# First product in float16 parts: split on ScalarE and VectorE, transposed by DMA, with the chunk's x norm in the taps

## The chip, the cores and the metric

The kernel runs on one core of a Trainium2 chip. The metric is the device time of one execution in microseconds (us), lower is better. Before the change it is 1389.54 us, the median of three runs (1389.52 to 1389.61).

## What is computed

`x` is 8 × 4160 rows of 192 floats, `weight_gen` holds 8 heads × 7 taps for each row. The two stages, cut to what matters:

```
# stage 1: a causal convolution of 7 taps with softmaxed weights, by head (24 columns each)
w   = softmax(weight_gen over its 7 taps)
att[s, head] = sum over k of w[s, head, k] * x[s - 6 + k, head]

# stage 2: two products with a normalized, self-gated softmax between them
h    = att @ w_in                       # 33280 x 192 times 192 x 1024
solu = h * exp(h - max(h)) / (sum(exp(h - max(h))) + 1e-9)
ln   = (solu - mean(solu)) / sqrt(var(solu) + 1e-6) * g_ln
out  = ln @ w_out                       # 1024 x 192
```

`w_in` and `w_out` arrive as 64-bit floats and are made into 32-bit ones on the chip.

## The kernel before

Each of the 128 partitions owns a run of 260 consecutive rows. A *tile* is one row of every partition, so there are 260 tiles of 128 rows. The taps and x are loaded by *chunks* of 4, 8, 8 and then 16 tiles.

**Stage 1** works on *groups* of four tiles (the first two groups have two). GpSimd (POOL) multiplies the seven shifted rows by their taps (L133), adds three pairs (L139) and then two pairs into `half` (L141). VectorE (DVE) adds the last two into `a` (`fin`, L366). The softmax of a chunk's taps has seven steps t0 to t6: DVE maximum (L112), POOL subtraction (L114), ScalarE (ACT) exponential (L118), DVE sum (L120), ACT and DVE for the reciprocal (L122, L124), POOL product (L126).

**The way into the first product**, by pairs of tiles: ACT doubles the last 64 columns of `a` (`dup`, L372). TensorE (PE) transposes four 128×128 blocks against an identity into the PSUM buffer `pa` (`xT`, L383). ACT rounds them to fp32r, a 32-bit type that PE multiplies in one pass (`xhi`, L391). What rounding lost, `x_lo`, is made for every other pair by a PE product with minus the identity and an ACT copy (`xn` L398, `xlo` L405), and for the other pairs by one DVE subtraction (`xld`, L412).

**The first product** of a tile (`mm1`) is twelve matmuls of 512 columns in fp32r: high × high, high × low and low × high, six with 128 rows (L422) and six with 64 rows that go in twos beside each other (L427). Its result `h`, 128 × 1024 in PSUM, has three buffers.

**Between the products**, for each tile: DVE takes the negated maximum (`max`, L441), a bound (`vb`, L445) and its reciprocal (`vr`, L450); ACT the exponential with its sum (`exp`, L454); DVE h × scale × exp with its mean (`solu`, L460); ACT the squares (`sq`, L466) and the float16 high half (`hi`, L473); DVE the float16 low half (`lo`, L477). Per four tiles, eight short steps f0 to f7 on ACT and DVE (L500 to L520) make the factor of the output rows. One DMA then transposes the two halves of a tile, 16 blocks of 128×128 (`tr`, L485).

**The second product** (`mm2`, L529) is 24 matmuls of 192 columns in float16; ACT scales the result out of PSUM (`out`, L540), and every four tiles are stored (L543).

**What sets the order.** Every engine executes its instructions in the order in which they are written. `issue_order` (L603) writes that order before anything runs: a list of steps with an engine, a cost in nanoseconds and the steps that they wait for, run through a small schedule in which each engine takes the step with the lowest tile number plus `URGENCY`. So an engine waits where a step's input comes later than that schedule had it. All DMAs are issued by SyncE (SP), in order too, through one queue. POOL can run ahead of the rest by as much as the buffers hold: `half` has two, `a` three groups.

Of the kernel before, what the change touches and what calls it, by code (L numbers as in the profile page):

```python
# [12 lines left out]
I32 = mybir.dt.int32  # L13
# [13 lines left out]
def tile_kernel(ctx: ExitStack, tc: tile.TileContext, x, weight_gen, w_in, w_out, g_ln, out):  # L27
# [17 lines left out]
    FH = FF // 2  # L45

# [53 lines left out]
    TAP_STEPS = 7  # L100

    def softmax_taps(c, step):
# [54 lines left out]
    ident = const.tile([P, P], F32, name="ident")  # L157
    make_identity(nc, ident)
# [74 lines left out]

    def first_rows(f, step):
        fs = slice(f * FH, (f + 1) * FH)
        if step < 3:
            first[f] = float_of_double(f, raw_a[:, f * FF : (f + 1) * FF], FH, step)
        elif step == 3:
            nc.scalar.copy(wa_hi[:, fs], first[f])
        elif step == 4:  # L240
            nc.vector.tensor_tensor(
                out=wa_lo[:, fs], in0=first[f], in1=wa_hi.bitcast(F32)[:, fs], op=ALU.subtract
            )
# [41 lines left out]
    def prepare_second(step, half=None):  # L285
# [8 lines left out]
        elif step == 5:  # L294
            second["total"] = ps_a.tile([P, 512], F32, name="pa")
            nc.tensor.matmul(second["total"][:, :NP], ones, sq, start=True, stop=True)
        elif step == 6:

            total = second["total"]
            tot = total[:, 8:9]  # L300
            k, kinv = (total.bitcast(I32)[:, n : n + 1] for n in (9, 10))
            nc.vector.tensor_reduce(tot, total[:, :NP], axis=AX.X, op=ALU.add)
            nc.vector.tensor_scalar(
                k, tot.bitcast(I32), 1, EXPONENT,
                op0=ALU.logical_shift_right, op1=ALU.bitwise_and,
            )
# [22 lines left out]
    a_of = {}  # L329
# [28 lines left out]
    def columns(t):  # L358
        return a_of[t // TG][:, t % TG : t % TG + group(t), :]

    def last_sum(t):
        if t % TG == 0:

            a_of[t // TG] = att.tile([P, TG, 2 * P], F32, name="a", bufs=3)
        half = half_of.pop(t)
        nc.vector.tensor_reduce(  # L366
            columns(t)[:, :, :D], half.rearrange("p j t d -> p t d j"), axis=AX.X, op=ALU.add
# [475 lines left out]
```

## Time and profile before

| | |
|---|---|
| Median of three runs | 1389.54 us |
| The profiled execution: its time, its span | 1389.4 us, 1387.5 us |
| Granted TensorE clock, mean | 0.991 |
| Busy: PE, POOL, DVE, ACT | 91%, 90%, 89%, 81% |
| DMA: bytes, mean rate | 210.43 MB, 152 GB/s |

The profile is of one execution. Its span starts with the first and ends with the last instruction; the execution's time is 1.9 us longer. An instruction's *busy* time runs from its start to its end; on DVE and ACT the last hundredths of a microsecond of one overlap the start of the next, and on PE the ends are modelled. *Idle before* a group of instructions is time in which its engine stood still ahead of them, with the instruction or DMA that ended it (the *releaser*). PEld is the load of weights into PE, which overlaps PE.

### The profile page before, as it was taken

To read this page: it belongs to the slowest core of one execution; us is meant where nothing else is said; L and a number is where in the kernel's file an instruction comes from. 1 tells how busy PE (TensorE), PEld (TensorE's weight loads), DVE (VectorE), ACT (ScalarE), POOL (GpSimd) and SP (SyncE) were. 2 spreads that over 40 slices of the span, in tenths; PEclk is the share of its full clock that TensorE was granted. 3 is DMA by queue.
4 is the path that set the end of the run, shared out by engine and by line. 5 is a ranking of instruction groups with operands and counts; after the bars stand their busy time and mean duration, and the time that the engine had idled before them with its cause. 6 is when DMAs were issued, how large, how long until landed. Compare 5 with 4: busy or idle time off the path is not lost.

```text
span 1387.5 us, 26562 instructions
## 1 busy us (share of the span) xinstructions
PE 1259.2 (91%) x10028; PEld 988.6 (71%) x10028; DVE 1230.0 (89%) x2068; ACT 1128.5 (81%) x2231; POOL 1247.0 (90%) x243
## 2 busy tenths in 40 slices
PE   0389899999999999989989999999999999999997
PEld 0267677777777777767767677777777777777776
DVE  2999898999989899889989898989899889999984
ACT  1588887888888888888888888888788888888885
POOL 1999999999999999999999999999999999999100
PEclk9989999999999999999999999999999999999999
DMA  3469768696968789697857768687858668766765
GB/s 90 139 142 194 147 128 201 124 207 122 194 130 174 146 145 195 122 198 123 186 130 166 158 149 186 118 190 145 193 109 191 146 140 176 132 133 117 134 131 116
DMA packets 565241, 210.43 MB, mean 152 GB/s; under 512 B 544329, under 2 KB 545785, under 8 KB 565112
## 3 DMA queue, kind: packets, MB, share of 16 engines
q1 hardware_dynamic: 565112, 208.73, 72.5%
q8 instruction: 79, 1.29, 0.4%
q14 instruction: 50, 0.41, 0.1%
HBM read 46.19 MB, written 25.56 MB: 52 GB/s over the span
## 4 chain that ended last, share of the span: by engine, by line
POOL 51%; DVE 16%; issue 13%; ACT 13%; PE 4%; DMA 3%; SPq 0%; POOLq 0%; DVEq 0%; ACTq 0%
POOL pr L133 27%; POOL pr L139 15%; POOL half L141 6%; DVE h L460 5%; ACT hl L473 4%; DVE hl L477 4%; ACT e L466 3%; DVE stats L441 3%; ACT e L454 3%; DVE a L366 3%; DMA xt<-in_x_dram 2%; POOL wt L114 2%; PE po L529 2%; POOL wt L126 1%; PE h L422 1%
## 5 line engine op out<-in xcount | busy, mean ns | idle before, releaser
L133 POOL TENSOR_TENSOR pr<-xt,wt 128x5376 f32<-128x5376 f32 (+1 forms) x66 | 631.3, 9565 | 23.1 <-DMA xt<-zeros 20.5
L529 PE MATMUL po<-w_hl,hlT 128*128 128x192 f16 x6192 | 558.5, 247 | 26.6 <-ACT ot L540 26.2
L529 PEld LDWEIGHTS <-hlT 128*128 128x128 f16 x6240 | 515.2, 98 | 82.2 <-issue 79.2
L477 DVE SCALAR_TENSOR_TENSOR hl<-h,hl 128x1024 f16<-128x1024 f32 x260 | 315.4, 1220 | 44.2 <-ACT e L466 31.5
L460 DVE SCALAR_TENSOR_TENSOR h<-h,stats,e 128x1024 f32<-128x1024 f32 x260 | 334.7, 1288 | 22.4 <-ACT e L454 9.2
L473 ACT ACTIVATE hl<-h 128x1024 f16<-128x1024 f32 x260 | 267.3, 1028 | 92.3 <-DVE stats L497 57.4
L139 POOL TENSOR_TENSOR pr<-pr 128x2304 f32<-128x2304 f32 (+1 forms) x66 | 332.7, 5041 | 5.2
L441 DVE TENSOR_REDUCE stats<-h 128x1 f32<-128x1024 f32 x260 | 316.1, 1216 | 8.9 <-PE h L427 8.1
L454 ACT ACTIVATE e<-h,stats 128x1024 f32<-128x1024 f32 x260 | 292.6, 1126 | 31.1 <-DVE stats L441 27.2
L466 ACT ACTIVATE e<-h,stats 128x1024 f32<-128x1024 f32 x260 | 292.3, 1125 | 5.9 <-DVE hl L477 5.4
L422 PE MATMUL h<-wa_hi,x_hi 128*128 128x512 f32 x520 | 225.4, 433 | 36.3 <-ACT e L466 22.8
L141 POOL TENSOR_TENSOR half<-pr 128x1536 f32<-128x1536 f32 (+1 forms) x66 | 225.8, 3422 | 5.2
L422 PE MATMUL h<-wa_hi,x_lo 128*128 128x512 f32 x520 | 207.5, 399 | 0.8 <-ACT x_lo L405 0.8
L422 PE MATMUL h<-wa_lo,x_hi 128*128 128x512 f32 x520 | 206.3, 397 | 0.0
L422 PEld LDWEIGHTS h<-wa_hi,x_hi 128*128 128x128 f32 x520 | 98.9, 190 | 59.3 <-ACT e L466 26.0
L427 PE MATMUL h<-wb_hi,x_hi 64*128 64x512 f32 x520 | 131.1, 500 | 0.0
L383 PE MATMUL pa<-ident,a 128*128 128x128 f32 x520 | 84.6, 286 | 44.2 <-DVE a L366 44.1
L540 ACT ACTIVATE ot<-po,stats 128x192 f32<-128x192 f32 x258 | 111.4, 432 | 8.5 <-PE po L529 8.5
L366 DVE TENSOR_REDUCE a<-half 128x768 f32<-128x1536 f32 (+1 forms) x66 | 116.4, 1764 | 1.6 <-POOL half L141 1.6
L427 PEld LDWEIGHTS h<-wb_hi,x_hi 64*128 64x128 f32 x520 | 48.6, 184 | 96.7 <-issue 96.7
L422 PEld LDWEIGHTS h<-wa_hi,x_lo 128*128 128x128 f32 x520 | 98.6, 190 | 24.3 <-ACT x_lo L405 1.6
L383 PEld LDWEIGHTS pa<-ident,a 128*128 128x128 f32 x520 | 55.8, 142 | 79.7 <-DVE a L366 44.1
(79 smaller groups left out, 1194.1 us busy)
## 6 DMA issues: line engine op xcount, KB each, us to landing
out_dram<-ot SPq DMA_DIRECT2D x65, 384.0 KB, 3.3
xt<-in_x_dram SPq DMA_DIRECT2D x30, 576.0 KB, 4.7
xt<-in_x_dram SPq DMA_DIRECT2D x30, 480.0 KB, 4.7
wt<-in_weight_gen_dram SPq DMA_DIRECT2D x15, 448.0 KB, 4.1
hlT<-hl SPq DMA_TRANSPOSE x260, 4.5
raw<-in_moe_w_out_dram SPq DMA_DIRECT2D x1, 1536.0 KB, 9.4
xt<-in_x_dram SPq DMA_DIRECT2D x3, 384.0 KB, 6.0
raw_a<-in_moe_w_in_dram SPq DMA_DIRECT2D x2, 512.0 KB, 11.5
```

What stands on the lines that cost most here:

```text
L133: nc.gpsimd.tensor_tensor(out=window(pr, 0, [(TG * D, K), (HG, n * H), (1, HG)]), in0=window(xt, t * D, [(D, K), (HG, n * H), (1, HG)]), i ...
L139: nc.gpsimd.tensor_tensor(out=pr[:, :3], in0=pr[:, :3], in1=pr[:, 3:6], op=ALU.add)
L141: nc.gpsimd.tensor_tensor(out=half, in0=window(pr, 0, [(2 * TG * D, 2), (D, n), (1, D)]), in1=window(pr, TG * D, [(5 * TG * D, 2), (D, n), ...
L422: nc.tensor.matmul(h[:, fs], lhs[:, 0, :], rhs[:, fs], start=n == 0, stop=False)
L427: nc.tensor.matmul(h[:, fs], lhs[rows, 1, :], rhs[rows], start=False, stop=n == 2,)
L441: nc.vector.tensor_reduce(stat(t, NMAX), h_of[t], axis=AX.X, op=ALU.max, negate=True)
L454: nc.scalar.activation(e, h_of[t], AF.Exp, bias=stat(t, NMAX), accum_out=stat(t, Z))
L460: nc.vector.scalar_tensor_tensor(out=h, in0=h, scalar=stat(t, SIGMA), in1=e, op0=ALU.mult, op1=ALU.mult, accum_out=stat(t, M))
L466: nc.scalar.activation(e_of.pop(t), h_of[t], AF.Square, bias=stat(t, M), scale=-float(FF), accum_out=stat(t, Q),)
L473: nc.scalar.activation(hl[:, 0, :], h_of[t], AF.Copy, scale=2.0**14)
L477: nc.vector.scalar_tensor_tensor(out=hl[:, 1, :], in0=h_of[t], scalar=2.0**14, in1=hl[:, 0, :], op0=ALU.mult, op1=ALU.subtract,)
L529: nc.tensor.matmul(po[:, :D], hlT[:, half * NJ + j, :], w2_hl[:, j, w, :], start=n == 0, stop=n == len(terms) - 1,)
```

## The change

**The first product in float16.** `att` is scaled by 2^14 and split into a float16 high and low part, and so is `w_in`, by a power of two found from the sum of its squares. The low × low part is dropped. High and low columns of a tile lie beside each other as 384 columns, three blocks of 128: the 64 last high columns share a block with the first 64 low columns, so that ten matmuls of 512 columns with 128 rows each are the whole product.

```
-        for fs in halves:
-            for n, (lhs, rhs) in enumerate(((hi, wa_hi), (hi, wa_lo), (lo, wa_hi))):
-                nc.tensor.matmul(h[:, fs], lhs[:, 0, :], rhs[:, fs], start=n == 0, stop=False)
...
+        terms = [(0, wa_hi), (0, wa_lo), (1, wb_hi), (1, wb_lo), (2, wc_hi)]
+        for f in range(2):
+            fs = slice(f * FH, (f + 1) * FH)
+            for n, (b, rhs) in enumerate(terms):
                 nc.tensor.matmul(
+                    h[:, fs], x3[:, b, :], rhs[:, fs], start=n == 0, stop=n == len(terms) - 1
                 )
```

**The way into it.** `fin` now writes a pair of tiles into PSUM (`pa`, one buffer); ACT writes the high part, DVE the low part, and one DMA on SP's queue transposes the six blocks of a pair into `xT` (four buffers). `dup`, the PE transposes, `xn`, `xlo` on ACT and `xld` are gone.

```
+        nc.vector.tensor_reduce(
+            pa, half.rearrange("p j t d -> p t d j"), axis=AX.X, op=ALU.add
+        )
+        part_of[t] = pa, small.tile([P, 2, 2 * D], F16, name="xhl", bufs=2)
+
+    def high_x(t):
+        pa, xhl = part_of[t]
+        nc.scalar.activation(xhl[:, :, :D], pa, AF.Copy, scale=S_UNIT)
+
+    def low_x(t):
+        pa, xhl = part_of[t]
+        nc.vector.scalar_tensor_tensor(
+            out=xhl[:, :, D:], in0=pa, scalar=S_UNIT, in1=xhl[:, :, :D],
+            op0=ALU.mult, op1=ALU.subtract,
+        )
...
+        nc.sync.dma_start_transpose(xT, xhl.rearrange("p t d -> p (t d)"))
```

**The norm of x.** So that float16 holds them, the taps of a chunk are divided by the root of the sum of squares of the chunk's x and of the chunk before (per partition). ACT squares a chunk's x in four instructions of 768 elements (L149; one for a short chunk), DVE adds (L155), ACT makes the power −1/2 by Ln and Exp (L160, L161), and a new step t6 multiplies it into the taps' reciprocal on ACT (L128), ahead of the POOL product, which is now t7 (L130). The factor back is `BACK`, used as the scale of `exp` and `solu`.

```
+            nc.scalar.activation(
+                junk[:, : (r1 - r0) * D].rearrange("p (t d) -> p t d", d=D), rows, AF.Square,
+                accum_out=squares_x[:, c + 1, part : part + 1],
+            )
...
+            nc.scalar.activation(row[:, LN], row[:, SUM], AF.Ln, bias=floor)
+            nc.scalar.activation(row[:, SIG], row[:, LN], AF.Exp, scale=-0.5)
```

**The row scale comes later.** ACT makes `SHIFT` = maximum × `BACK` (`nb`, L486) between `max` and `exp`; `vb` reads it, and the row's scale `vr` goes into `hi` and `lo` (until now 2^14) and no longer into `solu`. Of the steps per four tiles, six are left.

```
+    def shift(t):
+        nc.scalar.activation(stat(t, SHIFT), stat(t, NMAX), AF.Copy, scale=row(t, BACK))
...
-            out=h, in0=h, scalar=stat(t, SIGMA), in1=e, op0=ALU.mult, op1=ALU.mult, accum_out=stat(t, M)
+            out=h, in0=h, scalar=row(t, BACK_S), in1=e, op0=ALU.mult, op1=ALU.mult,
+            accum_out=stat(t, M),
...
-        nc.scalar.activation(hl[:, 0, :], h_of[t], AF.Copy, scale=2.0**14)
+        nc.scalar.activation(hl[:, 0, :], h_of[t], AF.Copy, scale=stat(t, SIGMA))
```

**The preparation of `w_in`** gets a sum of squares (ACT), a PE product and four short DVE steps for the power of two, and nine DMAs that put the rows of the blocks together, ahead of the first `mm1`.

**The order.** `URGENCY` is another table, and the steps have other costs and waits; among them:

```
-    a00=-79.4, a01=-110.4, a02=-10.4, a03=-9.5, a04=28.3, a10=35.2, a11=8.2, a12=-10.4, a13=2,
+    a00=-24.8, a01=-1.4, a02=311.9, a03=-96.8, a04=-123, a05=-44.2, a06=161.9, a10=70.9, a11=29.9,
...
-        add("attA", t, POOL, 14206 if full else 7302, *after, ready=21100 if c == 1 else 0)
-        add("attB", t, POOL, 3380 if full else 1764, ("attA", t), ("fin", groups[i - 2] if i > 1 else -1))
+        add("attA", t, POOL, 14990 if full else 7500, *after, ready=21100 if c == 1 else 12000)
+        done = [(f"fin", u + 2 if group(u) == 4 else u) for u in groups[i - 2 : i - 1] if i > 1]
+        add("attB", t, POOL, 3480 if full else 1800, ("attA", t), *done)
```

What this does to the order is shown at three places. Of the numbers behind a name, the higher is the buffer that was taken later in the written program.

First ACT at the start, where `w_in` (h, 128x512), the taps of the first chunks (wt 128x224 and 128x448, wy) and now their x (xt) are worked on. Before:

```order
L201 ACTIVATE h<-h 128x512
L202 ACTIVATE h<-h 128x512
L118 ACTIVATE wt<-wt 128x224
L122 ACTIVATE wy<-wm 128x32
L201 ACTIVATE h<-h 128x512
L202 ACTIVATE h<-h 128x512
L228 CAST wb_hi<-h 128x512
```

Now:

```order
L239 ACTIVATE h<-h 128x512
L240 ACTIVATE h<-h 128x512
L149 ACTIVATE junk,squares_x<-xt 128x1920
L120 ACTIVATE wt<-wt 128x224
L239 ACTIVATE h<-h 128x512
L240 ACTIVATE h<-h 128x512
L282 ACTIVATE e,sq<-h 128x512
L160 ACTIVATE row<-row,floor 128x1
L161 ACTIVATE row<-row 128x1
L124 ACTIVATE wy<-wm 128x32
L149 ACTIVATE junk,squares_x<-xt 128x1536
L128 ACTIVATE wy<-wy,row 128x32
```

The first chunk's tap scale (L128) now stands behind the squares of the x of chunk 0 (1920 elements) and of chunk 1 (1536 elements); before, nothing of the taps of chunk 0 stood behind a load of x.

Second POOL's last group (tiles 256 to 259), and DVE's maxima whose h buffer was taken just before and just after that group's `half`. Before, POOL and then DVE:

```order
L133 TENSOR_TENSOR pr_14931<-xt_13329,wt_12372 128x5376
L139 TENSOR_TENSOR pr_14931<-pr_14931 128x2304
L141 TENSOR_TENSOR half_14930<-pr_14931 128x1536
...
L441 TENSOR_REDUCE stats_129<-h_14865 128x1
L460 SCALAR_TENSOR_TENSOR h_14807,stats_129<-h_14807,stats_129,e_14882 128x1024
...
L441 TENSOR_REDUCE stats_129<-h_14935 128x1
```

Now:

```order
L172 TENSOR_TENSOR pr_14881<-xt_13222,wt_12282 128x5376
L178 TENSOR_TENSOR pr_14881<-pr_14881 128x2304
L180 TENSOR_TENSOR half_14880<-pr_14881 128x1536
...
L483 TENSOR_REDUCE stats_121<-h_14861 128x1
L507 SCALAR_TENSOR_TENSOR h_14809,stats_121<-h_14809,row_13584,e_14874 128x1024
...
L483 TENSOR_REDUCE stats_121<-h_14928 128x1
```

Before, h_14865 is the maximum of the 239th tile, so that 21 tiles' products are written behind POOL's last group; now h_14861 is the 250th, and 10 are. Counted the same way at tile 20 these leads are 9 and 10: before, POOL's lead grows through the program, now it stays.

Third DVE in the middle of the program, the work of two tiles. Before:

```order
L460 SCALAR_TENSOR_TENSOR h,stats<-h,stats,e 128x1024
L497 TENSOR_REDUCE stats<-stats 128x4
L441 TENSOR_REDUCE stats<-h 128x1
L477 SCALAR_TENSOR_TENSOR hl<-h,hl 128x1024 x2
L445 TENSOR_REDUCE stats<-stats 128x1
L412 TENSOR_TENSOR x_lo<-pa,x_hi 128x512
L450 RECIPROCAL stats<-stats 128x1
L460 SCALAR_TENSOR_TENSOR h,stats<-h,stats,e 128x1024
L497 TENSOR_REDUCE stats<-stats 128x4
```

Now:

```order
L483 TENSOR_REDUCE stats<-h 128x1
L490 TENSOR_REDUCE stats<-stats 128x1
L495 RECIPROCAL stats<-stats 128x1
L507 SCALAR_TENSOR_TENSOR h,stats<-h,row,e 128x1024
L483 TENSOR_REDUCE stats<-h 128x1
L436 TENSOR_REDUCE pa<-half 128x384
L525 SCALAR_TENSOR_TENSOR hl<-h,stats,hl 128x1024
L545 TENSOR_REDUCE stats<-stats 128x4
L490 TENSOR_REDUCE stats<-stats 128x1
L507 SCALAR_TENSOR_TENSOR h,stats<-h,row,e 128x1024
L495 RECIPROCAL stats<-stats 128x1
```

`fin` (L436) comes by pairs, in smaller pieces; `solu` (L507) no longer needs the reciprocal (L495) ahead of it, and `vb` (L490) now needs ACT's `nb` between it and the maximum (L483).

More of the change, by code (lines that the diff above doesn't have):

```diff
@@ new lines, in scale_first @@
+    def scale_first(step):
+        if step == 0:
+            first["total"] = ps_o.tile([P, 512], F32, name="po")
+            nc.tensor.matmul(first["total"][:, :3], ones, sq[:, 4:7], start=True, stop=True)
+        elif step == 1:
+            exponents(first["total"], 3)
+        elif step == 2:
+            k = first["k"] = small.tile([P, 1], F32, name="k", bufs=2)
+            nc.scalar.copy(k, first["total"][:, 9:10])
+            for n, factor in enumerate((1.0, S_UNIT)):
+                nc.scalar.activation(
+                    back[:, n : n + 1], first["total"][:, 10:11], AF.Copy, scale=factor
+                )
@@ L377, in transpose_x @@
     def transpose_x(t):
-        a = a_of[t // TG]
-        pa = ps_a.tile([P, 2, 2, P], F32, name="pa")
+        _, xhl = part_of.pop(t)
+        xT = small.tile([P, 6, P], F16, name="xT", bufs=4)
+        nc.sync.dma_start_transpose(xT, xhl.rearrange("p t d -> p (t d)"))
         for i in range(2):
-            for n in range(2):
-                nc.tensor.matmul(
-                    pa[:, n, i, :], a[:, (t + i) % TG, n * P : (n + 1) * P], ident,
-                    is_transpose=True, start=i == n == 0, stop=i == n == 1,
-                )
@@ L387, in transpose_x @@
-        x_parts[t] = [pa]
-    def high_x(t):
-        hi = small.tile([P, 2, 2, P], F32R, name="x_hi", bufs=2)
-        nc.scalar.copy(hi, x_parts[t][0])
-        x_parts[t].append(hi)
-    def subtract_high(t):
-        pa, hi = x_parts[t]
-        for n in range(2):
-            nc.tensor.matmul(
-                pa[:, n], minus, hi[:, n], start=False, stop=n == 1, skip_group_check=True
-            )
-    def low_x(t):
-        pa, hi = x_parts.pop(t)
-        lo = small.tile([P, 2, 2, P], F32R, name="x_lo", bufs=2)
-        nc.scalar.copy(lo, pa)
-        for i in range(2):
-            xt_of[t + i] = hi[:, :, i, :], lo[:, :, i, :]
@@ L554, in tile_kernel @@
     ops = dict(
-        attA=attend, attB=lambda t: None, fin=last_sum, dup=copy_columns, xT=transpose_x,
-        xhi=high_x, xn=subtract_high, xlo=low_x, xld=low_x_on_vector, mm1=first_product,
-        max=maximum, vb=bound, vr=row_scale, exp=exponentials, solu=solu, sq=squares, hi=high_half, lo=low_half,
-        tr=transpose_s, mm2=second_product, out=finish, od=store, lw=at_chunk(load_w),
-    )
-    for n in range(5):
-        ops[f"b{n}"] = once(last_rows, n)
-    for n in range(5):
-        for f in range(2):
-            ops[f"a{f}{n}"] = once(first_rows, f, n)
+        attA=attend, attB=lambda t: None, fin=last_sum, xhi=high_x, xlo=low_x, xT=transpose_x,
+        mm1=first_product, max=maximum, nb=shift, vb=bound, vr=row_scale, exp=exponentials,
+        solu=solu, sq=squares, hi=high_half, lo=low_half, tr=transpose_s, mm2=second_product,
+        out=finish, od=store, lw=at_chunk(load_w),
+    )
+    for part in range(3):
+        for n in range(7):
+            ops[f"a{part}{n}"] = once(convert_first, part, n)
+    for n in range(3):
+        ops[f"s{n}"] = once(scale_first, n)
     for n in range(3):
```

340 lines of the change are left out of this document (190 added, 150 removed).

## Prediction

> **What bounds the kernel now.** I read the page's sum first, then the span cut into stages, then the groups of instructions between 300 and 1200 us, where nothing of the start or the end is left.
>
> ```profile
> PE 1259.2 (91%) x10028; PEld 988.6 (71%) x10028; DVE 1230.0 (89%) x2068; ACT 1128.5 (81%) x2231; POOL 1247.0 (90%) x243
> ```
> ```profile
> 300.00:600.00 300.00, 286.34 (x2308) 225.02 (x2305) 277.13 (x462) 255.36 (x503) 296.94 (x56) 1.00 0.79 159
> 600.00:900.00 300.00, 282.56 (x2268) 221.51 (x2267) 272.77 (x454) 251.20 (x494) 297.02 (x55) 0.99 0.75 156
> 900.00:1200.00 300.00, 286.43 (x2291) 225.25 (x2290) 273.44 (x459) 254.42 (x502) 296.78 (x54) 0.99 0.75 158
> 1290.00:1340.00 50.00, 49.32 (x396) 38.50 (x395) 44.27 (x78) 42.34 (x86) 0.00 (x0) 1.00 0.65 122
> ```
> ```profile
> L141 POOL TENSOR_TENSOR half<-pr 128x1536 f32<-128x1536 f32 x47 | 163.2, 3472 | 3.7
> L441 DVE TENSOR_REDUCE stats<-h 128x1 f32<-128x1024 f32 x178 | 216.3, 1216 | 3.5 <-PE h L427 2.9
> L118 ACT ACTIVATE wt<-wt 128x896 f32<-128x896 f32 x11 | 10.5, 952 | 30.3 <-POOL wt L114 30.3
> L366 DVE TENSOR_REDUCE a<-half 128x768 f32<-128x1536 f32 x47 | 84.2, 1791 | 1.6 <-POOL half L141 1.6
> L412 DVE TENSOR_TENSOR x_lo<-pa,x_hi 128x512 fp32r<-128x512 f32 x45 | 30.7, 682 | 0.3 <-ACT x_hi L391 0.2
> L497 DVE TENSOR_REDUCE stats<-stats 128x4 f32<-128x8 f32 (+1 forms) x179 | 28.0, 157 | 11.9 <-ACT stats L516 5.4 <-ACT e L466 3.7 <-ACT stats L500 2.1
> L391 ACT CAST x_hi<-pa 128x512 fp32r<-128x512 f32 x89 | 52.6, 591 | 3.4 <-PE pa L383 3.4
> L405 ACT CAST x_lo<-pa 128x512 fp32r<-128x512 f32 x44 | 26.3, 598 | 0.6 <-PE pa L398 0.5
> L372 ACT COPY a<-a 128x256 f32<-128x256 f32 x47 | 19.4, 413 | 11.0 <-DVE a L366 10.9
> L504 ACT ACTIVATE stats<-stats 128x4 f32<-128x4 f32 x45 | 9.3, 208 | 1.1 <-DVE stats L497 1.1
> ```
>
> In a window the columns behind its length are the busy times of PE, PEld, DVE, ACT and POOL. In these 900 us POOL is busy 890.7 (99%), PE 855.3 (95%), DVE 823.3 (91%), ACT 761.0 (85%). In the same 900 us POOL finishes 47 groups, 188 tiles; DVE takes the maximum of only 178. So two rates run beside each other: POOL's 4.79 us per tile, and 5.06 for the three engines behind it, which I call the consumers. POOL never stops, its lead grows, and it is through early:
>
> ```profile
> 31.59 4.95 POOL L133 TENSOR_TENSOR pr<-xt,wt 128x2688 f32<-128x2688 f32 x1 [20.46 <-DMA xt<-zeros]
> 52.54 9.70 POOL L133 TENSOR_TENSOR pr<-xt,wt 128x5376 f32<-128x5376 f32 x1
> 1284.98 3.48 POOL L141 TENSOR_TENSOR half<-pr 128x1536 f32<-128x1536 f32 x1
> ```
>
> From its first full group at 52.5 to its end at 1288.5 it takes 1235.9 us for 256 tiles, 4.83 each with the taps. Then 99.0 us pass to the end of the span. PE has hardly a gap in the window behind POOL's end (49.3 of 50), at 5.0 us per tile:
>
> ```profile
> 1290.00:1340.00 50.00, 12.18 (x10) 1.00 0.65 122
> ```
>
> That is the same window for DVE's maximum alone, ten in 50 us. So PE sets the consumers' rate. A second loss is the tap exponential, L118 above: ACT stood still 30.3 us in these 900 for POOL's L114, 11 times. The written order wants POOL further ahead at every chunk (leads of 9 tiles at the start and 21 at the end), and where POOL is not yet there ACT stops, with DVE and PE behind it:
>
> ```profile
> 694.62 1.74 POOL L114 TENSOR_TENSOR wt<-wt,wm 128x896 f32<-128x896 f32 x1
> 696.39 0.95 ACT L118 ACTIVATE wt<-wt 128x896 f32<-128x896 f32 x1 [4.55 <-POOL wt L114]
> 698.49 0.79 PE L422 MATMUL h<-wa_hi,x_hi 128*128 128x512 f32 x1 [4.35 <-ACT e L466]
> ```
>
> **The change part by part, per tile.**
>
> *PE.* Two tiles show the pieces: a first product begins at 1285.04, its matmuls follow each other by 0.23 us, and the second product begins at 1287.41; the transposes of a pair begin 0.49 ahead of a second product.
>
> ```profile
> 1285.04 0.39 PE L422 MATMUL h<-wa_hi,x_hi 128*128 128x512 f32 x1
> 1285.27 0.39 PE L422 MATMUL h<-wa_lo,x_hi 128*128 128x512 f32 x1
> 1287.41 2.15 PE L529 MATMUL po<-w_hl,hlT 128*128 128x192 f16 x24
> 1282.05 0.66 PE L383 MATMUL pa<-ident,a 128*128 128x128 f32 x4
> 1282.54 2.15 PE L529 MATMUL po<-w_hl,hlT 128*128 128x192 f16 x24
> ```
>
> Ten float16 matmuls of 512 columns are not in the trace. The fp32r row gives 0.23 each; the float16 rows of the second product give 2.15/24 for 192 columns, 0.24 for 512. So 2.30 to 2.39 in place of 2.37: nothing gained there. The transposes (0.49/2) and `xn` (half as often, under 0.1) go. PE needs 2.30 + 2.15, some 4.5 with gaps, where it was busy 855.3/178 = 4.81.
>
> *DVE* was busy 823.3/178 = 4.63. Off: `xld` 0.682/4 = 0.17, `fin` 1.791/4 = 0.45, one short step 0.157/4 = 0.04. On: `fin` by pairs, two of 0.96 per four tiles (the half group in the row below), 0.48; `xlo`, 384 elements, by the row of 564 ns, 0.28; two short steps per chunk, 0.02. Sum 4.75. That its output goes to PSUM may cost or save a little; I take nothing.
>
> ```profile
> 43.07 0.96 DVE L366 TENSOR_REDUCE a<-half 128x384 f32<-128x768 f32 x1
> ```
> ```profile
> L209 DVE SCALAR_TENSOR_TENSOR h<-raw,h 128x384 int32<-128x384 int32 x4 | 2.3, 564 | 0.1
> L202 ACT ACTIVATE h<-h 128x384 int32<-128x384 int32 (+1 forms) x7 | 3.6, 521 | 0.2
> ```
>
> *ACT* was busy 761.0/178 = 4.28. Off: `dup` 0.413/4, `xhi` 0.591/2, `xlo` 0.598/4, a short step 0.208/4: 0.60. On: `nb` 0.21; `xhi` of 384 elements, by a row that mixes 384 and 512, at most 0.52/2 = 0.26; four squares per 16 tiles, each under the 0.95 of 896 elements plus 0.21 for its sum, 0.29; small steps of the norm, 0.07. Sum 4.51 at most.
>
> *POOL* keeps its instructions: 4.83. It is now the fullest engine, then DVE (98% of 4.83), ACT and PE (93%). What hid behind PE's 5.0 is no longer hidden.
>
> *The added wait.* `vb` on DVE waits for `nb` on ACT, and `solu` and `lo` queue behind it. The bound is 0.21 plus the handoffs per tile if nothing covers it; the exponential (ACT, over 1 us) stands beside it, and DVE has a `lo` or a `fin` between in the pieces shown, so I take nothing. Where `vr` follows `vb` and `solu` no longer waits for `vr`, DVE gains as much.
>
> *SP.* Each pair puts six blocks into the queue in which 16-block transposes, x, taps and output stand in order:
>
> ```profile
> hlT<-hl SPq DMA_TRANSPOSE x260, 4.5
> ```
> ```profile
> q1 hardware_dynamic: 565112, 208.73, 72.5%
> ```
>
> In the window 1290 to 1340 the DMA share was 0.65 with ten such transposes and some output: at most 3.3 us of all engines each, so 1.2 for six blocks, 0.6 per tile, on 0.725 × 1387.5/260 = 3.9. Over 5.2 us per tile that is 86%. A pair's way (`fin`, `xhi`, `xlo`, transpose) is some 7 us and `xT` holds four pairs, three ahead, 29 us: hidden. The Trainium skill (VectorE: DVE Perf Modes, The three transpose paths and Rules for kernel authors) speaks against this step: 390 ns on TensorE, 1309 ns by DMA for 128×128, and TensorE wherever PSUM will do. By that, as an estimate, a pair waits 7.9 us instead of the trace's 4.5 for 16 blocks, which the 29 us still cover.
>
> *The order.* At POOL's end 10 tiles are behind it in place of 21. That takes 11 × 5.0 = 55 of the 99.0 us, leaving 44.0.
>
> *The start.* POOL began at 31.59, when the zeros behind x landed. Now the first tap scale (L128) stands behind the squares of chunk 1's x. That load is issued between these two:
>
> ```profile
> raw<-in_moe_w_out_dram SPq DMA_DIRECT2D x1, 1536.0 KB, 9.4
> xt<-xt SPq DMA_DIRECT2D x1, 576.0 KB, 7.3
> ```
> ```profile
> 30.57 0.43 SPq L173 DMA_DIRECT2D raw<-in_moe_w_out_dram  x1
> 31.67 4.71 SPq L85 DMA_DIRECT2D xt<-in_x_dram  x1
> 36.48 0.55 SPq L86 DMA_DIRECT2D xt<-xt  x1
> ```
>
> So it lands between 30.6 + 9.4 = 40.0 and 36.5 + 7.3 = 43.8; I take 41.5. The square of 1536 elements (by the 952 ns of 896, 1.6), its sum, the scale and the tap product are 2.8: POOL begins at 44.3, 12.7 later (11 to 15). The work on `w_in` with its nine DMAs grows too, but its first product is not what POOL waits for.
>
> *Sum.* POOL's end 1288.5 + 12.7 = 1301.2; the rest 44.0; and 8 because consumers this full will not keep 4.83 evenly (4.83 to 4.90 over 256 tiles is 0 to 18). Span 1353.2, and 1.9 around it as in the profiled execution (1389.4, at the median): **1355**.
>
> **Rivals.**
> - *DVE sets the rate at 4.95.* It would be 96% busy, as PE was. 0.12 × 256 = 31 on 1301.2 + 44.0 + 1.9 gives 1378. For it: max, `nb`, `exp`, `solu`, `hi`, `lo` cross between DVE and ACT five times. Against: three `h` buffers, and the ACT stops at L118 should go.
> - *Slower: the way over ACT.* DVE was idle 0.43 per tile ((900 − 823.3)/178). If `nb` stands behind long ACT instructions in each tile, DVE keeps that idleness: 4.75 + 0.43 = 5.18, 0.35 × 256 = 90, 1437. It turns slower at 4.83 + (1389.5 − 1347.1)/256 = 5.00, an idleness of 0.25. Against: part of the 0.43 is PE's and L118's doing.
> - *Slower too: transposes stuck behind x loads.* If each of 15 chunk loads stops PE once for 4.35 us, like the stop shown, 1347 + 65 = 1412. Against: the 29 us.
> - *The change does little*, since ten matmuls cost what twelve did. True of the product itself; then only the transposes and the order pay, and the DVE rival is what that looks like.
>
> **How the numbers follow.** Forecast 0.56 (its own range 1340 to 1368), DVE at 4.95 0.24 (1368 to 1386), no change 0.05, way over ACT 0.10, stuck transposes 0.05. So faster 0.80, same 0.05, slower 0.15; 0.2% is about what a measurement of this kernel can tell. The range goes from 1340 (POOL's start 11 later, no unevenness) to 1400, short of the two slower cases.
>
> **What would show it.** Right: POOL 98% busy with its last instruction near 1301, 44 to 55 us behind it, DVE near 4.75 busy per tile, no stop at the tap exponential after the start, PE under 94%. Wrong: POOL with stops (then taps or `half` wait for ACT or DVE); PE's first matmul waiting for `xT` (the DMA); DVE's `vb` waiting for `nb` over 0.2 us per tile; a first product well off 2.3 us.

## The result, and the profile after

The kernel after takes **1460.14 us** (median of 4 runs, 1457.52 to 1463.66), the kernel before 1389.53 beside it: a ratio of 1.0512, 95% interval 1.0488 to 1.0537. The forecast was 1355 and faster; it came out 105 us above that, outside the range and on the other side. The profiled execution has a span of 1459.5 us and a granted clock of 0.968.

The page's sum of the kernel after, and the chain that ended last:

```profile
PE 1154.7 (79%) x8860; PEld 787.0 (54%) x8860; DVE 1258.2 (86%) x2172; ACT 1231.4 (84%) x2518; POOL 1241.6 (85%) x241
...
ACT 32%; DVE 20%; issue 14%; PE 12%; DMA 6%; SPq 1%; ACTq 0%; DVEq 0%
```

No engine is over 86% busy any more, and the chain, half POOL in the kernel before, now has no POOL in it: it changes between ACT, DVE, PE and DMAs. The stages of the middle (busy PE, PEld, DVE, ACT, POOL, then clock, DMA share and GB/s):

```profile
300.00:600.00 300.00, 249.07 (x1895) 167.64 (x1893) 264.85 (x456) 262.05 (x534) 279.38 (x51) 0.97 0.86 172
600.00:900.00 300.00, 250.60 (x1960) 171.33 (x1958) 270.68 (x464) 264.49 (x539) 264.90 (x50) 0.98 0.82 165
900.00:1200.00 300.00, 250.66 (x1899) 171.77 (x1898) 263.03 (x453) 261.24 (x536) 274.08 (x51) 0.95 0.86 172
```

In the groups of instructions of these 900 us stand DVE's maximum, POOL's `half` and the tap exponential on ACT:

```profile
L483 DVE TENSOR_REDUCE stats<-h 128x1 f32<-128x1024 f32 x171 | 207.8, 1215 | 17.4 <-PE h L466 17.2
...
L180 POOL TENSOR_TENSOR half<-pr 128x1536 f32<-128x1536 f32 x43 | 147.8, 3438 | 3.4
...
L120 ACT ACTIVATE wt<-wt 128x896 f32<-128x896 f32 x10 | 9.5, 950 | 0.0
```

171 tiles in 900 us are 5.26 us per tile, for the consumers and now for POOL too (43 groups, 172 tiles). DVE and PE need no more busy time than forecast: 798.55/171 = 4.67 (forecast 4.75) and 750.3/171 = 4.39 (4.5). ACT needs 787.8/171 = 4.61, 0.10 above its "at most 4.51". None of these reaches 5.26; the rest is idle time between the instructions: DVE had 0.43 of it per tile, and has 0.59. POOL's way through the program:

```profile
44.63 4.94 POOL L172 TENSOR_TENSOR pr<-xt,wt 128x2688 f32<-128x2688 f32 x1
...
65.56 9.71 POOL L172 TENSOR_TENSOR pr<-xt,wt 128x5376 f32<-128x5376 f32 x1
...
1390.59 3.43 POOL L180 TENSOR_TENSOR half<-pr 128x1536 f32<-128x1536 f32 x1
```

It begins where it was forecast (44.3) and ends at 1394.0 in place of 1301.2. The waits of the same 900 us (total us, times, longest):

```profile
PE po L573 <- ACT ot L584: 74.6, 61, 5.5
POOL wt L116 <- DVE wm L114: 55.3, 8, 11.0
...
ACT junk L149 <- DMA xt<-in_x_dram: 27.4, 15, 4.5
ACT stats L486 <- DVE stats L483: 25.6, 35, 2.3
PE h L466 <- DVE hl L525: 24.5, 20, 3.4
...
PE h L466 <- DMA xT<-xhl: 14.3, 8, 4.5
...
DVE stats L490 <- ACT stats L486: 10.3, 6, 4.0
```

POOL waits for DVE's tap maximum (L114), which stands in DVE's order behind consumer steps that are late; PE waits for ACT's copy out of the one `po` buffer. I read both as results of the pace: in the run without the three costs below, which keeps 4.81 us per tile, POOL's wait falls to 2.8 us, and PE's, 55.1 us there, does no harm. Two waits are for a DMA: ACT's squares for the load of x, and PE's first product for `xT`. How one such stop runs on through the engines, in order of time:

```profile
577.65 0.55 DVE L447 SCALAR_TENSOR_TENSOR xhl<-pa,xhl 128x384 f16<-128x384 f32 x1
...
579.43 3.99 SPq L533 DMA_TRANSPOSE hlT<-hl  x1
...
583.51 1.24 SPq L455 DMA_TRANSPOSE xT<-xhl  x1
...
584.81 0.57 SPq L92 DMA_DIRECT2D xt<-in_x_dram  x1
...
588.16 4.45 PE L466 MATMUL h<-w,xT 128*128 128x512 f16 x10 [4.47 <-DMA xT<-xhl]
...
589.61 0.84 ACT L149 ACTIVATE junk<-xt 128x768 f32<-128x768 f32 x1 [2.74 <-DMA xt<-in_x_dram]
...
592.65 1.23 DVE L483 TENSOR_REDUCE stats<-h 128x1 f32<-128x1024 f32 x1 [4.38 <-PE h L466]
```

The pair's `xlo` (L447) is done at 578.2, but SP first issues a store, a load and a transpose of the two halves of a tile (`hlT`, 4 us), then this transpose of x at 583.5, and only then the next load of x, at 584.8. PE had just used up the pair before, so none of the three pairs that the prediction counted ahead was there. PE stands 4.47 us for its `xT` and then takes 4.45 us for the ten matmuls, nearly twice what they take here, after a shorter stop:

```profile
510.12 2.33 PE L466 MATMUL h<-w,xT 128*128 128x512 f16 x10 [1.28 <-DVE hl L525]
```

ACT stands at the squares until 589.6, with an `out`, `hi` of two tiles and a `sq` behind them, and DVE waits 4.38 for PE. All three consumers have stopped within 6 us.

### The profile page after: what moved, and what is told of

The parts are those of the page before. It is cut to its first block, busy times and chain, and to the rows that moved or that the text cites. A ratio compares the mean times of both kernels' runs of the same rounds, so it can differ in the third digit from the quotient of the medians.

```text
span 1459.5 us, 24942 instructions
## 1 busy us (share of the span) xinstructions
PE 1154.7 (79%) x8860; PEld 787.0 (54%) x8860; DVE 1258.2 (86%) x2172; ACT 1231.4 (84%) x2518; POOL 1241.6 (85%) x241
## 4 chain that ended last, share of the span: by engine, by line
ACT 32%; DVE 20%; issue 14%; PE 12%; DMA 6%; SPq 1%; ACTq 0%; DVEq 0%
ACT hl L521 9%; ACT e L514 8%; ACT e L499 8%; DVE hl L525 6%; PE h L466 6%; PE po L573 5%; DVE stats L483 5%; DVE h L507 4%; DMA xt<-in_x_dram 4%; ACT ot L584 2%; ACT stats L486 2%; DVE pa L436 2%; DMA xT<-xhl 1%; ACT junk L149 1%; DVE xhl L447 1%
## 5 line engine op out<-in xcount | busy, mean ns | idle before, releaser
L466 PE MATMUL h<-w,xT 128*128 128x512 f16 x2600 | 624.8, 390 | 125.1 <-DMA xT<-xhl 35.2
L466 PEld LDWEIGHTS <-xT 128*128 128x128 f16 x2600 | 250.1, 100 | 416.4 <-issue 77.8
L525 DVE SCALAR_TENSOR_TENSOR hl<-h,stats,hl 128x1024 f16<-128x1024 f32 x260 | 331.6, 1278 | 63.6 <-ACT e L514 33.1
L507 DVE SCALAR_TENSOR_TENSOR h<-h,row,e 128x1024 f32<-128x1024 f32 x260 | 334.1, 1285 | 29.6 <-ACT e L499 26.9
L483 DVE TENSOR_REDUCE stats<-h 128x1 f32<-128x1024 f32 x260 | 315.9, 1215 | 21.2 <-PE h L466 20.4
L514 ACT ACTIVATE e<-h,stats 128x1024 f32<-128x1024 f32 x260 | 291.1, 1120 | 33.0 <-DVE stats L495 29.8
L499 ACT ACTIVATE e<-h,stats,row 128x1024 f32<-128x1024 f32 x260 | 314.1, 1208 | 2.6
L521 ACT ACTIVATE hl<-h,stats 128x1024 f16<-128x1024 f32 x260 | 288.7, 1117 | 26.5 <-DVE h L507 19.8
L436 DVE TENSOR_REDUCE pa<-half 128x384 f32<-128x768 f32 x130 | 125.8, 968 | 0.7
L486 ACT ACTIVATE stats<-stats,row 128x1 f32<-128x1 f32 x260 | 77.2, 297 | 45.2 <-DVE stats L483 44.7
L149 ACT ACTIVATE junk<-xt 128x768 f32<-128x768 f32 (+2 forms) x63 | 55.8, 885 | 68.7 <-DMA xt<-in_x_dram 46.7
L447 DVE SCALAR_TENSOR_TENSOR xhl<-pa,xhl 128x384 f16<-128x384 f32 x130 | 71.0, 547 | 1.4 <-ACT xhl L443 1.4
L490 DVE TENSOR_REDUCE stats<-stats 128x1 f32<-128x2 f32 x260 | 37.5, 147 | 20.2 <-ACT stats L486 19.6
```

The source lines that it names most:

```text
L436: nc.vector.tensor_reduce(pa, half.rearrange("p j t d -> p t d j"), axis=AX.X, op=ALU.add)
L466: nc.tensor.matmul(h[:, fs], x3[:, b, :], rhs[:, fs], start=n == 0, stop=n == len(terms) - 1)
L483: nc.vector.tensor_reduce(stat(t, NMAX), h_of[t], axis=AX.X, op=ALU.max, negate=True)
L499: nc.scalar.activation(e, h_of[t], AF.Exp, bias=stat(t, SHIFT), scale=row(t, BACK), accum_out=stat(t, Z))
L507: nc.vector.scalar_tensor_tensor(out=h, in0=h, scalar=row(t, BACK_S), in1=e, op0=ALU.mult, op1=ALU.mult, accum_out=stat(t, M),)
L514: nc.scalar.activation(e_of.pop(t), h_of[t], AF.Square, bias=stat(t, M), scale=-float(FF), accum_out=stat(t, Q),)
```

## The experiments

The theory formed from this: three steps that the prediction priced at nothing or by their busy time alone (the squares of x, the scales read from memory, the transposes of x on SP's queue) cost the time, because every engine takes its steps in the written order and that order was written with other durations. Rivals: one of the three costs it all; the order itself is a bad draw; the consumers cannot keep 4.83 whatever is taken out.

The times of before beside these runs were 1388.9 to 1389.4 (medians on each chip). The ratios are to them.

### The order alone, on the kernel before

```
-        add("attA", t, POOL, 14206 if full else 7302, *after, ready=21100 if c == 1 else 0)
-        add("attB", t, POOL, 3380 if full else 1764, ("attA", t), ("fin", groups[i - 2] if i > 1 else -1))
+        add("attA", t, POOL, 14990 if full else 7500, *after, ready=21100 if c == 1 else 0)
+        add("attB", t, POOL, 3480 if full else 1800, ("attA", t), ("fin", groups[i - 2] if i > 1 else -1))
```

and 13.5 n in place of 13 n for POOL's two tap steps (n: a chunk's tiles times heads).

> The kernel before, with nothing but the costs of POOL's steps in the table that writes the order set to those of the change (a group 18.5 us in place of 17.6, the tap steps 13.5 in place of 13 ns per element). POOL's lead in the written order then stays at 9 to 11 tiles in place of growing from 9 to 21. Theory 'order' (the prediction's term of 55 us for the shorter tail): the stops of ACT at the tap exponential (39.6 us) go, 10 tiles fewer stand behind POOL's end, 1335 to 1365 us. Rival 'consumers': PE sets 5.0 us per tile whatever the lead is, a shorter lead only turns POOL's early end into stops of POOL, 1375 to 1392 us.

**1362.47 us**, ratio 0.9809 (0.9792 to 0.9825): faster than both kernels. Its groups in the 900 us:

```profile
L441 DVE TENSOR_REDUCE stats<-h 128x1 f32<-128x1024 f32 x186 | 225.9, 1214 | 0.0
...
L118 ACT ACTIVATE wt<-wt 128x896 f32<-128x896 f32 x11 | 10.5, 953 | 0.0
```
```profile
sum 900.00, PE 883.40 PEld 691.29 DVE 849.25 ACT 783.05 POOL 890.67; mean PE 294.47 PEld 230.43 DVE 283.08 ACT 261.02 POOL 296.89
```

The stop at the tap exponential is gone (30.3 to 0.0), and the old consumers do 186 tiles, 4.84 us each, close to POOL's 4.83; PE is 98% busy with 883.4/186 = 4.75 per tile. So before the change it was not PE's 5.0 that held the consumers at 5.06: it was the order. What PE saved by the change was not needed for this pace; it would be for one below 4.75, where the old PE is full.

### One cost out at a time, the order of after kept

Squares left out from the third chunk on, where a constant stands for their sums:

```
+            if c > 1:
+                return
-    nc.vector.memset(squares_x, 0.0)
+    nc.vector.memset(squares_x, 8.0)
```

> The change, same order, but the squares of x on ACT are left out from the third chunk on (the sums of squares are a constant, so the taps are scaled by another norm). Theory 'loads': ACT stands 46.7 us behind x loads at these squares and takes everything with it; with the instructions (0.23 us per tile) gone, 1390 to 1420 us. Theory 'longer hand-over' (per-row scales make exp and hi longer and nb stands between max and exp): ACT's waits move elsewhere, 1440 to 1455 us.

Scales as constants in the instructions:

```
-            e, h_of[t], AF.Exp, bias=stat(t, SHIFT), scale=row(t, BACK), accum_out=stat(t, Z)
+            e, h_of[t], AF.Exp, bias=stat(t, SHIFT), scale=7.84 * 2.0**-24, accum_out=stat(t, Z)
-        nc.scalar.activation(hl[:, 0, :], h_of[t], AF.Copy, scale=stat(t, SIGMA))
+        nc.scalar.activation(hl[:, 0, :], h_of[t], AF.Copy, scale=2.0)
-            out=hl[:, 1, :], in0=h_of[t], scalar=stat(t, SIGMA), in1=hl[:, 0, :],
+            out=hl[:, 1, :], in0=h_of[t], scalar=2.0, in1=hl[:, 0, :],
```

> The change, same order, but the scales of exp, hi and lo are constants of the program in place of values per row in memory (so the result is scaled otherwise, and hi no longer waits for vr). Theory 'longer hand-over': exp falls from 1.21 to 1.13 us, hi from 1.12 to 1.03, lo from 1.28 to 1.22, all in the chain of a tile between DVE and ACT; 0.17 to 0.23 us per tile, 1400 to 1420 us. Theory 'loads': 1440 to 1455 us.

Transposes of x left out, the first product reads one constant tile:

```
-        nc.sync.dma_start_transpose(xT, xhl.rearrange("p t d -> p (t d)"))
+        xT = xT_const
```

> The change, same order, but the DMA transposes of x are left out and every first product reads the same constant tile (the output is then not that of x). Theory 'loads' in its second form (transposes of x are late behind the queue; PE waits 35 to 46 us for them and comes back at the lower clock): 1400 to 1425 us, clock back near 0.99. Theory 'longer hand-over': under 15 us gained, 1445 to 1460 us.

Without squares **1409.81** (ratio 1.0147, 1.0127 to 1.0167), with constant scales **1430.11** (1.0293, 1.0272 to 1.0314), without transposes **1423.98** (1.0249, 1.0226 to 1.0271): 50, 30 and 36 us of the 1460. None is the whole cause, and none is nothing. The scales gained less than was expected if they were the cause (1400 to 1420) and more than if they were not. Without the transposes the granted clock was 0.974 in the profiled execution, not "near 0.99".

### Wait or work: the squares

```
+            if c > 1:
+                rows = ones.unsqueeze(1).broadcast_to([P, 6, P])
```

> The kernel after in its own order, only that from the third chunk on ScalarE squares a tile of constants of the same 768 elements, so that it has the same work but nothing to wait for from x's load (the norms are then not those of x). Leaving the squares out took 1460 to 1410. If ScalarE's stop for the load (46.7 us in the whole run, 23 times) was what they cost, this run is at 1410 to 1420 too. If their busy time was (1.05 us each, 0.26 per tile), it stays at 1450 to 1460.

**1420.91** (1.0227, 1.0209 to 1.0245). The work is all there:

```profile
L153 ACT ACTIVATE junk<-ones 128x768 f32<-128x768 f32 x44 | 37.9, 862 | 0.1
L153 ACT ACTIVATION_READ_ACCUMULATOR junk<-ones 128x1 f32 x44 | 9.6, 218 | 0.0
```

With the same 44 squares and no load to wait for, 39 of the 50 us are gone. That is about what the stops amount to: in the whole run of the kernel after, ACT stands 46.7 us at the squares for loads of x, 5.9 of it at the first two chunks, whose squares stayed as they were here.

```profile
L149 ACT ACTIVATE junk<-xt 128x768 f32<-128x768 f32 (+2 forms) x63 | 55.8, 885 | 68.7 <-DMA xt<-in_x_dram 46.7
```

So a stop of ACT here costs the kernel about its own length. The busy time of 0.26 per tile costs some 11.

### Wait or queue: the transposes of x

```
-            xt_of[t + i] = xT[:, 3 * i : 3 * i + 3, :]
+            xt_of[t + i] = xT_const[:, 3 * i : 3 * i + 3, :]
```

> The kernel after in its own order; the DMA transposes of x are issued as before, but the first product reads one constant tile (its output is not that of x), so the queue carries the same and TensorE never waits for it. Leaving the transposes out altogether took 1460 to 1424. If TensorE's waits for xT cost that (35.2 us, 17 times), this run is at 1420 to 1430 too, and the squares still wait for x's load. If it was the load on the queue, by which x came later (ScalarE's stops for x fell from 27.4 to 5.8 us of the 900 in the middle), it is at 1445 to 1460.

**1452.39** (1.0454, 1.0432 to 1.0475). PE's wait for `xT` is worth 8 of the 36 us; 28 are lost by issuing the transposes at all. With each issued twice, the second into a tile that nobody reads:

```
+        again = small.tile([P, 6, P], F16, name="again", bufs=2)
+        nc.sync.dma_start_transpose(again, xhl.rearrange("p t d -> p (t d)"))
```

> The kernel after in its own order, with every transpose of x issued twice, the second into a tile that nobody reads. Issuing the transposes without TensorE waiting for them cost nearly all that they cost (1452 against 1424). If it is the issue on SyncE's queue (1.4 us each by SyncE's rows) and the room on the DMA engines, a second costs as much again: 1485 to 1510. If the queue has room left, 1455 to 1470.

**1492.93** (1.0751, 1.0723 to 1.0779): 33 us more, so as much again. ACT's stops at the squares of x in the 900 us, without the transposes, with them unread, and with them twice:

```profile
ACT junk L149 <- DMA xt<-in_x_dram: 5.8, 6, 2.8
```
```profile
ACT junk L149 <- DMA xt<-in_x_dram: 25.1, 15, 3.8
```
```profile
ACT junk L149 <- DMA xt<-in_x_dram: 43.7, 18, 5.6
```

5.8, 25.1 and 43.7 us (27.4 in the kernel after): with the transposes the loads of x come late for the squares, on the one queue that issues both. A load's own time from issue to landing hardly grows with them (median 4.6 us for the larger pieces, 4.4 without), which leaves its issue as what is late. SP is late in two ways: its rows for a transpose of x last 1.2 to 2.0 us, and it stands for their input (36.9 us for `xlo` in the 900 us of the kernel after). The second transpose of each pair has its input ready, so the doubled run speaks for the rows themselves. The share of the DMA engines rises as well (0.72 to 0.75, 0.82 to 0.88, 0.92 to 0.94 in the three stages of these runs); queue and engines were not taken apart. So part of what the transposes cost is paid at the squares. How large that part is, no run shows by itself.

### Wait or length: the scales

```
-        nc.scalar.activation(hl[:, 0, :], h_of[t], AF.Copy, scale=stat(t, SIGMA))
+        nc.scalar.activation(hl[:, 0, :], h_of[t], AF.Copy, scale=two)
```

and the same for `lo`, with `two` a constant column in memory.

> The kernel after in its own order, with the scale of hi and lo read from a constant column in memory (so s is scaled by a constant); the exponential keeps its row scale. Constants in the instructions gained 30 us of 1460, with shorter instructions and without hi's wait for vr. If the wait for vr was what cost it, 1430 to 1440 here; if it is the longer instructions (0.08 to 0.09 us each on ScalarE, 0.06 on VectorE), 1452 to 1463.

**1458.72** (1.0492, 1.0473 to 1.0510): no gain. The wait of `hi` and `lo` for the row's scale costs nothing, which leaves the length of the instructions for the 30 us. The rows of `hi`, `exp` and `lo` with constants in the instructions, and after:

```profile
L525 DVE SCALAR_TENSOR_TENSOR hl<-h,hl 128x1024 f16<-128x1024 f32 x260 | 315.6, 1216 | 52.8 <-ACT hl L521 27.9 <-ACT e L514 23.3
...
L499 ACT ACTIVATE e<-h,stats 128x1024 f32<-128x1024 f32 x260 | 290.6, 1118 | 2.5
L521 ACT ACTIVATE hl<-h 128x1024 f16<-128x1024 f32 x260 | 265.2, 1027 | 27.6 <-DVE h L507 20.1 <-DVE stats L545 4.8 <-DVE stats L490 1.3
```
```profile
L525 DVE SCALAR_TENSOR_TENSOR hl<-h,stats,hl 128x1024 f16<-128x1024 f32 x260 | 331.6, 1278 | 63.6 <-ACT e L514 33.1 <-ACT hl L521 27.7
...
L499 ACT ACTIVATE e<-h,stats,row 128x1024 f32<-128x1024 f32 x260 | 314.1, 1208 | 2.6
...
L521 ACT ACTIVATE hl<-h,stats 128x1024 f16<-128x1024 f32 x260 | 288.7, 1117 | 26.5 <-DVE h L507 19.8 <-DVE stats L545 4.3 <-DVE stats L490 1.3
```

With a scale from memory 90 ns are added to each of the two ACT instructions and 62 ns to DVE's: 0.24 us per tile, 63 us of engine time over 260 tiles, of which 30 show.

### All three out

> The kernel after in its own order without the squares of x, with constant scales, and without the transposes of x (output not that of x). The three single runs sum to 50 + 30 + 36 = 116 us. If the three costs add up and nothing else is lost, 1340 to 1350, which is also where the sum of the prediction lay. If they share the same idle time, or the order written for other durations is a loss of its own, 1365 to 1400.

**1355.31** (0.9760, 0.9746 to 0.9775), between the two ranges that were expected.

```profile
L487 DVE TENSOR_REDUCE stats<-h 128x1 f32<-128x1024 f32 x187 | 226.9, 1214 | 3.2 <-PE h L470 2.8
```
```profile
sum 900.00, PE 797.34 PEld 552.37 DVE 857.27 ACT 792.11 POOL 886.75; mean PE 265.78 PEld 184.12 DVE 285.76 ACT 264.04 POOL 295.58
```
```profile
1298.14 3.44 POOL L182 TENSOR_TENSOR half<-pr 128x1536 f32<-128x1536 f32 x1
```

187 tiles in the 900 us, 4.81 each, and POOL through at 1301.6, the place of the forecast. DVE is 95% busy there and keeps the pace. The single gains sum to 116 us, together they are 105, so they nearly add; and these three are what stands between the forecast and the result. As they nearly add, the time that the transposes cost can be the same as the squares' wait only to a small part, some 11 us if nothing offsets it. That the time equals the forecast is partly chance, since this kernel lacks work that the forecast counted.

### The order written with other numbers

ACT's and DVE's costs raised by what the trace shows above them (`exp` 1091 to 1173, `hi` 910 to 995, `nb` 100 to 190, `lo` 1135 to 1193, squares 800 to 950), all work done:

> The kernel after, complete, with the planner's costs of ScalarE and VectorE raised by what the trace shows above them: exp 1091 to 1173, hi 910 to 995, nb 100 to 190, lo 1135 to 1193, squares of x 800 to 950; the order is then worked out anew. If the order written for shorter instructions is what loses the time, 1400 to 1440. If the instructions, the loads and the waits themselves lose it, 1450 to 1465.

Squares planned 5 us after the landing of x, and 10 us after it:

```
-            gap = 0 if e == SP else SAME[e] if engine == e else CROSS
+            gap = 5000 * (name[:2] == "lx" and engine == ACT) if e == SP else SAME[e] if engine == e else CROSS
```

> The kernel after, complete; the planner counts 5 us more from the landing of x to the squares of x, so ScalarE meets them later, with x there; the order is worked out anew. If what the squares cost is ScalarE standing in order for x's load (constant squares gained 39 us of 1460), 1415 to 1435, with the stop at junk near 0. If any new order does no better than the one on record, 1445 to 1465.

> As the run before it, with 10 us instead of 5: tells whether the gain comes from the load's wait or from a chance order. By the wait: the same time within some 10 us, 1415 to 1435, with no stop at junk. By chance of the order: anywhere from 1420 to 1470.

Both, raised costs and 5 us:

> The kernel after, complete, with both: the raised costs of ScalarE and VectorE (1445 by itself) and squares 5 us after x's landing. If the two losses are separate they add: 1395 to 1415. If they are the same idle time of ScalarE and VectorE, 1415 to 1440.

Raised costs **1444.89** (1.0406, 1.0391 to 1.0422); squares 5 us later **1440.68** (1.0369, 1.0354 to 1.0385), 10 us later **1445.88** (1.0405, 1.0390 to 1.0421); both **1396.99** (1.0050, 1.0035 to 1.0065). Raised costs alone came out between their two ranges. Later squares fell short of their expectation: the stop at `junk` is gone, but other waits take its place. In the runs with 5 and with 10 us:

```profile
PE h L466 <- DMA xT<-xhl: 23.4, 11, 4.0
...
POOL wt L130 <- ACT wy L128: 17.4, 6, 8.7
```
```profile
POOL wt L130 <- ACT wy L128: 47.0, 9, 13.1
...
PE h L466 <- DMA xT<-xhl: 28.3, 15, 4.2
```

POOL's tap product now waits for the tap scale, which needs the norm: squares that come later make POOL late instead, 47 us at 10. Together the two edits gain 63, more than their 15 and 19. One reason shows in the run with raised costs alone, where ACT's stop at the squares had grown from 27.4 to 40.4 us in the 900:

```profile
ACT junk L149 <- DMA xt<-in_x_dram: 40.4, 20, 3.5
```

In the run with both edits it is gone. That run's groups and waits:

```profile
L483 DVE TENSOR_REDUCE stats<-h 128x1 f32<-128x1024 f32 x180 | 218.4, 1214 | 9.2 <-PE h L466 8.9
```
```profile
POOL wt L116 <- DVE stats L490: 8.6, 3, 3.5
...
PE h L466 <- DMA xT<-xhl: 4.5, 2, 3.6
```

```profile
600.00:900.00 300.00, 258.57 (x2029) 178.00 (x2028) 279.36 (x483) 275.57 (x567) 290.32 (x55) 0.98 0.91 179
```

5.00 us per tile; the long waits for DMAs and of POOL are nearly gone, and the DMA share is 0.91. Two further edits on top of it:

```
+ gap of 1500 from xT to its first product
```

> The kernel after, complete, as the run with both corrections (1397), and the planner counts 1.5 us more from a transpose of x to its first product. If what is left above 1355 is TensorE waiting for xT, 1375 to 1390; if not (the two waits for xT in that run's 900 us were 4.5 us), 1392 to 1405.

```
-            free[e], end = time + 60, data + 950
+            free[e], end = time + (2400 if name == "tr" else 1400 if name == "xT" else 550), data + 950
```

> The kernel after, complete, as the run with both corrections (1397), and the planner takes SyncE as occupied 2.4 us by a transpose of s, 1.4 by one of x and 0.55 by another transfer, as SyncE's rows show, where it took 0.06. If what is left above 1355 is the queue that is behind its plan, 1370 to 1390; if the rest is lost elsewhere, 1392 to 1410.

**1417.74** (1.0207, 1.0192 to 1.0223) and **1394.48** (1.0037, 1.0026 to 1.0049). The first made it worse, beyond both its ranges; the second is the same within 3 us. Neither finds the rest.

### Controls: any other order

One cost, DVE's maximum, is moved by 3 ns, which rewrites much of the order and puts nothing right in it: after with 1143 and with 1137 for 1140, and before with 1134 for 1131. In the written orders 1321 and 1317 of ACT's 1784 steps behind the preparation of the weights then stand at another place, and in the third 522 of 1603.

> The kernel after, complete, with one planner cost changed by next to nothing (the maximum 1140 to 1143) and nothing corrected: a control for what any other order gives. If the gains of the corrected orders come from the corrections, 1450 to 1470. If the order on record is a bad draw that any new one mends, 1395 to 1440.

> The same control in the other direction (1140 to 1137). By the corrections 1450 to 1470; by chance of the order anywhere from 1395 to 1470, and then some 20 us from the run before it.

> The kernel before, complete, with the same small change (the maximum 1131 to 1134): a control for the 27 us that POOL's raised costs gained. If the shorter lead gained them, 1385 to 1395 here; if any new order gains, 1355 to 1380; if the order of before is a good draw among many, 1395 to 1420.

**1462.42** (1.0524, 1.0509 to 1.0540), **1462.39** (1.0524, 1.0508 to 1.0539) and **1388.56** (0.9995, 0.9985 to 1.0005). In these three a new order by itself changes nothing, so the gains above are put down to the numbers that were put in. For the kernel before the control is the weaker one: one run, and a third of the steps moved.

## Why the prediction was wrong

**The step that failed** is the last term of the sum: "and 8 because consumers this full will not keep 4.83 evenly (4.83 to 4.90 over 256 tiles is 0 to 18)". The consumers keep 5.26 in the middle 900 us. POOL ends 92.8 us later than forecast, where 8 were allowed: 0.36 per tile over 256 tiles. Its reason failed too: without the three costs DVE is 95% busy and keeps 4.81. What was missing in the sum are three costs, taken as hidden or not seen:

- *The squares.* They were priced as 0.29 us of busy time per tile, and have 0.26 (0.85 + 0.20 for each of four per 16 tiles). That they read a load which lands 4.6 us after its issue, and that everything behind them on ACT then stands, was not priced. 39 of their 50 us are that wait.
- *The transposes of x*, "hidden" by three pairs ahead. On PE they nearly were: 8 us, though the three pairs were not always ahead. The other 28 us are lost by issuing them at all, and the forecast left out what they are queued ahead of: the loads of x behind them on SP, and by these the squares on ACT, are the part that the traces show. Where most of the 28 us is paid stays open. The forecast did work out the DMA share of 86% (0.82 to 0.86 came) and drew nothing from it. The Trainium skill (VectorE: DVE Perf Modes, Rules for kernel authors) gives the transposes to TensorE wherever PSUM will do. The runs agree as far as they go: the DMA transposes cost 36 us, and the same by TensorE was not tried in this kernel. The latency that was estimated from that page was not the cause: six blocks land 3.0 us after their issue (median), not 7.9.
- *The scales.* The prediction named where the new scale goes and gave it no price. It costs 0.18 us per tile on ACT, more than the 0.10 by which it passed its bound, and 0.06 on DVE. The trace of before had no scale from memory at 1024 elements on ACT, but the price of a column could be read in it: `exp` (L454), whose bias is a column, took 98 ns more than `hi` (L473), which has none. They differ in function and output type as well.

```profile
L454 ACT ACTIVATE e<-h,stats 128x1024 f32<-128x1024 f32 x260 | 292.6, 1126 | 31.1 <-DVE stats L441 27.2
...
L473 ACT ACTIVATE hl<-h 128x1024 f16<-128x1024 f32 x260 | 267.3, 1028 | 92.3 <-DVE stats L497 57.4
```

The Trainium skill has the price too (ScalarE: Activation LUTs, What ACT_TABLE_LOAD costs): each operand read by partition adds some 93 ns to an activation. The rows agree: 90 ns for `exp` and `hi`.

**The order's 55 us** were mis-sized. It put 21 tiles behind POOL's end, as they stand in the written order. In the runs DVE's maximum came 17 times behind POOL's end before, and 10 times after:

```profile
1288.46:1387.50 99.04, 19.78 (x17) 0.98 0.65 124
```
```profile
1394.02:1459.50 65.48, 12.13 (x10) 1.00 0.73 146
```

So 7 tiles went, not 11, and 65.5 us were left in place of 44.0. With the 92.8 at POOL's end and the 8 that were already counted, 92.8 + 21.5 − 8 = 106.3 is the whole way from the 1353.2 to the span of 1459.5.

**What bounds the kernel** was half right. POOL's 4.83 was the floor. But "PE sets the consumers' rate" at 5.0 was read from a stretch in which the order, not PE, made the pace: the first experiment runs the same PE work at 4.84. A PE that is busy 49.3 of 50 us could still do more: its busy time was 4.93 per tile there and 4.75 in that run. Most of the gain that the prediction hoped for, 27 of 34 us, could be had without the change, and the change then had only its costs to give.

**Right were** the start (44.63 for 44.3), the first product (2.33 us in the row shown, 624.8/260 = 2.40 on the average, for 2.30 to 2.39), the busy times of DVE and PE within 0.11, the end of the stops at the tap exponential (0.0), and, by the kernel without the three, POOL's 4.83 as the pace.

**The rivals.** "The way over ACT" came nearest in time: DVE with its old idleness, 5.18 and 1437, where 4.67 + 0.59 = 5.26 came. Its mechanism was another. DVE's `vb` waits for `nb` 10.3 us in 900, 0.06 per tile, far from the 0.2 that the prediction set as its mark. "Transposes stuck behind x loads" had the queue right and the direction wrong in the main: the loads are stuck behind the transposes, and PE's waits for `xT` are worth 8 us.

**What stays open.** With the raised costs and later squares the complete kernel takes 1394 to 1397, no faster than before. Some 40 us remain above the kernel without the three. The longer instructions, the squares' own work and the DMA share of 0.91 are candidates; how it divides was not settled. Another queue for x, or earlier loads of it, were not tried.

## What to carry to other kernels

In an order that is fixed beforehand, price a step by what it waits for and by what stands behind it on its engine and its queue, not only by its busy time: the squares cost 11 us by their work and 39 by their wait. When the durations change, give the planner the measured ones before judging the change: here that, with later squares, was worth 63 us. And test the order of the kernel before on its own first: here it alone gave 27 us, and no complete kernel with the change was faster than before.

## What the hardware showed that was not expected

- ACT activations whose scale is a column in memory took 81 to 90 ns longer than those with a constant: 1208 for 1118 and 1117 for 1027 ns at 1024 elements, and the one-element `nb` 297 where a step of four elements with a constant scale takes 216. On DVE a scalar from memory added 62 ns (1216 to 1278).

```profile
L486 ACT ACTIVATE stats<-stats,row 128x1 f32<-128x1 f32 x260 | 77.2, 297 | 45.2 <-DVE stats L483 44.7
...
L552 ACT ACTIVATE stats<-stats 128x4 f32<-128x4 f32 (+1 forms) x67 | 14.5, 216 | 1.7 <-DVE stats L545 1.7
```

- SP's rows for a transpose are long: 4.0 us for 16 blocks and 1.2 for six in the rows shown (1.5 to 4.8 and 1.2 to 2.0 between 300 and 1200 us), where a load of x has 0.57. What follows in its queue is issued that much later.
- The stop of 4.47 us on PE was followed by a product at half speed: 4.45 us for ten matmuls in place of 2.33. The granted clock was 0.95 to 0.98 in the three stages, where it was 0.99 to 1.00 before.
